# Retention and token/channel mixer on one core: query scaled ahead of the products, sums kept in PSUM, half-array states

## The chip, the core and the metric

The kernel runs on one core of a Trainium2 chip. The core has a matrix engine (PE, which loads a stationary operand and streams a moving one past it, results to PSUM), three engines for elementwise work (DVE, ACT, POOL), a queue engine (SP), an on-chip memory of 128 partitions (SBUF) and eight PSUM banks of 128 partitions x 2 KB. Engines run side by side, each its own instructions in order, and wait for each other by semaphores. The metric is the device time of one execution in microseconds; less is better.

## The reference

Four batches, eight heads of 64, sequence 768. A retention layer with a decaying state per head is followed by a mixer over tokens and then over channels (relu in both, each with a residual):

```
gamma = 1 - 2 ** (-5 - h)                       # per head h
for t in range(768):
    state = gamma * state + outer(k[t], v[t])
    y[t]  = q[t] @ state / sqrt(64)
x  = y, heads side by side                      # (4, 768, 512)
u  = x + (relu(x.T @ w_tok1) @ w_tok2).T        # 768 -> 256 -> 768 over tokens
out = u + relu(u @ w_ch1) @ w_ch2               # 512 -> 1536 -> 512 over channels
```

## The kernel before

The recurrence is done in six chunks of 128 tokens. With gk and gy (powers of gamma inside a chunk, the second with the scale 1/8) a chunk's output is the masked product of its own queries and keys times v, plus its queries times the state that the chunks before it left.

`front(b, p)` does one pair of heads of one batch (16 calls), up to the transposed mixer input:

- The loads bring q, k, v as 16 bit numbers from POOL's queue (L446, L451, L453); `k16` is k times gk, in two halves by head (L500, L502).
- `turn` transposes k and q, in mode "t" or "w" on PE (L526, L528) with a copy from PSUM (L542), or "x" as a DMA on SP (L515). `TURNS` says which for each pair.
- State: five products of a whole chunk's 128 key columns by 128 value columns (L558); only the two 64x64 blocks on the diagonal are wanted. DVE adds them up with decay gp in U, 128 columns wide (L568, L570); L582/L584 copy the two blocks, decayed, into `r16`, whose other blocks are zero.
- Own chunk: six products of 64 partitions for each head (L603), the two heads on the two halves of the array, into four banks; a mask is applied on the way to `am` (L630, or L616 and L621).
- Outputs, in two half sequences: L644 (q times the state, 128 rows) and L647 (mask product times v, 64 columns) sum in a bank; L660/L664 scale by gy into X, L677 casts X to x16.
- Token mixer: L688, relu L697, L713 into new banks; L720 adds to X in place, L728 casts to u16, which is transposed into uT (L747 with copy L753, or L737 on SP).

`back(b)` does the channel mixer: `widen` makes 12 x 2 products of four parts each (L782) with relu on ACT (L798) into h; `narrow7` does the second product for two blocks of 128 tokens by seven half products instead of eight (L857, L872, L889, L905); the last two blocks take the plain `narrow` (L819, L828).

PSUM banks are shared: `first` (pairs of batch 0) any of the eight, `front` banks 0 to 5, `back` 4 to 7.

Order: each piece of work is an `Op` with the engines that could do it, an estimated cost for each, what it depends on and which slots it takes. `arrange` places them in time by these estimates, always the ready one first that ranks first in `PRECEDENCE`, a written-out order of all Ops in base 36. That fixes each engine's order of instructions and, where two engines could do an Op, which does. `ORDER` is the order of the loads. Where the plan leaves PE idle early on, products of zeros (L993) fill 70% of the gap.

Of the kernel before, what the change touches and what calls it, by code (L numbers as in the profile page):

```python
# [91 lines left out]
def arrange(ops, BUFS, BANKS, rank):  # L92
# [158 lines left out]
PRECEDENCE = (  # L251
    "ib89l7she55gqkr3jefy9cua01r20nup4i8rom1du264e9b91rgim2f38v3fmyb265uh27q2sr4c1mmssur5en66gdrgp6iktn9k02jynv4p"
    "et729nbcaj4dc7ow2g0aijo655tcffgjvkr1eo56r89o3q1lj719344n1g4mo1pj883ba6f1wkmwp8pi8gl0uebxlb4hdng83wcydeh3mth0"
    "hdk1j5bt6bgo3js983o081tp8txgcdekl5hqwcma3m7m280ibbkntgank3fqvxbn5br47iaev7dccmdvwbb4985xgmsqcrx53ys5bjm6bu7l"
    "blcugt8no5vb7nrrvmdoe0js8jfirjokcf09v5l6kzwydhins72m9y0ym7rkw9dxj1s1e6ewskq8hpl2brwwwzq16z590vbseampjxcw6q2p"
    "d0e3wrnw9uwjhgprhj62s2iy43sy3em8lv9ilf2cn5hm6sj2ty5f1n7akg8q82gxmni2n72lvjdgad2r060us40hpmis5yceu868hbx9ddx8"
    "fzh66uc0h9osbqwf000f0ewm33tzru8lhxfeudhlm49hmzcibfhffoarrz7shzed3zdsxapb0d04o3ihf8baai99hsmht9k8f43kcpav7bni"
    "ojw39lbvipsoppf98knrclb663b5m37kjlakidccq073gz4v17hohu2wvyiwlrfd1j0rejmi7x97memqlckilw2h8x716ljjoc1ag0w716xd"
    "i76fjd2qthhy1yat7w5ve7onei7znz6dqfm1gs7uvri610lxscopsl8haxtbi95alyivjhh5d81cpl18abugke5dev3uc4hcp2t4pvx6emts"
    "cj3o70401f846pa2erperdoqfm8putju5cbmc6xid7rf80xhd47r3c6i2nxlj4pyasezefwsmfhn0k13ol96vl57i444i3c8rwnyitpko7te"  # L260
    "0zeqjp36aqx4a47ci02aqb6aqqfsbzkm4sfx5448oesm5hcslib08u79ehkyxkft6tw222eg7gwo5mpdcx2vssqapwbko237gko99e5rvglm"
    "3xha0cszd3mj8e1vw6a7xmpxfcwlq56odz9zecg6i1b1lqstamhr126v0ox2mbgfgr7o9gl34anummoi2yqi6hkj50b7c2wiiiva35ctmovz"
    "xe11uj1b3npsjcqybhqgex6986bd7dmdlnd2e1t3d5n8p1nat523hemlpokk31383houic9fka9mve91q33d90rc7jczxjg4klmcdyiopztd"
    "j6qlalnsflrmdmuw2jc3fabg4b77ey1w9x9vpu4wgaqvta92h8lhk94tigsnngr0loilckpntvogn6imkfirbejrj0ixll471kwda0by253s"
    "v4f68zm0j9dbiffbcow5vt6r455jh13iqcvo9w0qja4zf7cajw8aiuodqxrq26034jtqrnu5uq4fkokt8yeusgmxnmlu15w0a8ndtwwta9lp"
    "gwbprsdi08remu3aov1ohhohus619qg73gvhf0vd5prp0l8m5qmvk4pfq6n3g5gv140pm9xbesqnmg2eu4ltse6cg12kqtf2r67tpg0sc9p9"
    "5idunpj34oq941qdncvst8mknxd6c132uztml4jg5278ge8c0gwua1daepljpq6w4rqojih2cn1ix38fqz4ghivuuy5zqraop04649df24qs"
    "nb7407izrxdr7eggrlee2ulan9le76w1a5n1r9quphqewxg98i95sv8o580jdt6xrosbkvjnjzjke8raac5s2i200bjodp1pt7xfu1sdt69t"
    "k6si75ls676k7pc56ne4elq7p4j8qp4epte2oo7q9jk7uk8bl1n4f5u7sa9dub1x2bn0mrfgtfk55krtnlbod1h7g2njwvv1s3gltltx2zo4"
    "cqcv2db3fnchvntu6yjfuv60jt8wgp9bjvdjqjausfu0az1zun2ot0oa3vnqfria9aucq4w8qmtka31ucbk0u63rgqkxhkfk2ft2obfwoyvq"  # L270
    "050wsxumay5t42urr7gcx0o8gnuld9dwawebs6tjrvkr0t5lwhkcrhuuv22tu393wp3lksv9jq87trfhvw4x4u0xvck2wauiotv0gu6jb8vf"
    "9pry53v8t1kw4qlkgbvp4kbw0mpato7vfpl8ofufoxagv6bikughs894aftiu9wgfuuxviqh9r396euoh4lzsjahrb8dri6mfjxcs0ie4y5e"
    "kbttkdlg1en2nti55op51t3pcg6gldht7ykqwedqjm215uwqnkm5khkp7h2xhvg39sozfvor4lpcx1nhjbl91sne3twnx7vv295n2siqdlnf"
    "8s1hsw511qv3dkp385apaaqwnonnp7spgy305w7fi8hww4"
# [4 lines left out]
def kernel(  # L279
# [31 lines left out]
    BUFS = dict(kf=1, k=4, q=4, v=4, k16=3, kT=4, qT=4, U=2, r16=3, am=8, X=3, x16=4, h1=5, u16=3,  # L311
# [14 lines left out]
    HARD = {(0, 0, "k")}  # L326
    ops = []
# [31 lines left out]
    gy = const_p.tile([P, H], FP, name="gy")  # L359
    gp = const_p.tile([P, NP], FP, name="gp")  # L360
    ident16 = const_p.tile([P, P], F16, name="ident16")
    mask = const_p.tile([P, 1, P], FP, name="mask")
    gyw = const_p.tile([P, H, D], FP, name="gyw")
    zero = const_p.tile([P, 384], F16, name="zero")
    NR = BUFS["r16"]
    r16 = [const_p.tile([P, NC - 1, P], F16, name=f"r16_{i}") for i in range(NR)]
# [26 lines left out]
    def emit():  # L393
        for p in range(NP):
            nc.vector.memset(gp[:D, p:p + 1], g128[2 * p])
            nc.vector.memset(gp[D:, p:p + 1], g128[2 * p + 1])
    gp_op = prep("DVE", 600, emit, prio=(-20, 0, -1, 1))
# [3 lines left out]

    def emit():
        for t in r16:
            nc.vector.memset(t, 0.0)
    r16_op = prep("DVE", 1000, emit, prio=(-20, 0, -1, 2))
# [31 lines left out]
    def load(b, p, what):  # L437
# [3 lines left out]
        chunks = what == "q" and not wide  # L441
        s = Slot("kf" if hard else what)

        def emit():
            if wide:
                nc.gpsimd.dma_start(out=tile_of(s, [P, 2, NC, D], F16).rearrange("p h c d -> p h (c d)"),  # L446
                                    in_=src.rearrange("h (p c) d -> p h (c d)", c=NC))
            elif chunks:
                t = tile_of(s, [P, NC, 2, D], F16)
                for j in range(2):  # L450
                    nc.gpsimd.dma_start(out=t[:, :, j], in_=src[j].rearrange("(c p) d -> p c d", p=P))  # L451
            else:
                (nc.sync if hard else nc.gpsimd).dma_start(out=tile_of(s, [P, 2, NC, D], FP if hard else F16),  # L453
                                                           in_=src.rearrange("h (c p) d -> p (h c) d", p=P))
# [4 lines left out]
        else:  # L459
            o = request((-20, 0, b, p), 1660 if chunks else 710 if wide else 1030, emit, dma, [s])  # L460
        loads[b, p, what] = (s, o)

    def front(b, p):
# [10 lines left out]
        def parts(emit, costs, deps, slot, src, steps):  # L474
            got = []
            for st in steps:
                def put(e, st=st):
                    emit(e, st)
                got.append(op(either(put, **costs), deps, [] if got else [slot],
                              ([slot] if got else []) + [src], behind=got[-1] if got else None))  # L480
            return got

        def half(hf):
            return slice(hf * HC, (hf + 1) * HC)

        X, UT = Xs[b], UTs[b]
        pc = slice(p * P, (p + 1) * P)
        (KF, kd), (Q, qd), (V, vl) = (loads[b, p, x] for x in "kqv")
        K = Slot("k16")
# [5 lines left out]
        def emit(e, js):  # L495
            t = opened(K, [P, NC, 2, D], F16)
            for j in js:
                h = 2 * p + j
                if e == "ACT":
                    nc.scalar.activation(t[:, :, j], KF.tile[:, j], AF.Copy, scale=gk[:, h:h + 1])  # L500
                else:
                    (nc.vector if e == "DVE" else nc.gpsimd).tensor_scalar(t[:, :, j], KF.tile[:, j], gk[:, h:h + 1],  # L502
                                                                           None, ALU.mult)
        kl = parts(emit, dict(ACT=(506, 610), DVE=(335 if (b, p, "k") in HARD else 265, 420), POOL=(450, 510)),
                   [kd, g_op], K, KF, ([0], [1]))

        def flat(t):
            return t.rearrange("p c h d -> p (c h d)")

        def turn(src, dst, dep):  # L510
            mode = TURN[b, p, "q" if dst is QT else "k"]
            if mode == "x":
                def emit():
                    t = tile_of(dst, [P, S], F16)
                    nc.sync.dma_start_transpose(out=t.rearrange("d (c t) -> d c t", t=P),  # L515
                                                in_=flat(src.tile))
                o = Op(ops, (PLACE[b, p], 0, b, p, 0), [("SP", 1200, 1200, emit)], dep, [dst], [src], dma=(48, 24))
                return [o, o]
            T = Slot(FA)

            def emit():
                tp = tile_of(T, [P, 1024], F16)
                for c in range(NC):
                    if mode == "w":
                        for j in range(2):
                            nc.tensor.transpose(tp[j * D:(j + 1) * D, c * P:(c + 1) * P], src.tile[:, j, c], ident16)  # L526
# [3 lines left out]
            t = op(one("PE", (465, 530) if mode == "w" else (340, 500), emit), dep + [ident_op], [T], [src])  # L530

            def emit(e, hs):
                d, o = opened(dst, [P, S], F16), T.tile[:, :S]
                if mode == "w":
                    d = d.rearrange("d (f p c) -> d f p c", f=2, c=NC)[:, hs]
                    o = o.rearrange("d (c f p) -> d f p c", f=2, c=NC)[:, hs]
                else:
                    d = d.rearrange("d (f t) -> d f t", f=2)[:, hs]
                    o = o.rearrange("d (f t) -> d f t", f=2)[:, hs]
                if mode == "w" and hs == slice(0, 2):  # L540
                    d, o = d.rearrange("d f p c -> d (f p) c"), o.rearrange("d f p c -> d (f p) c")
                (nc.scalar.copy if e == "ACT" else nc.vector.tensor_copy)(d, o)  # L542
            slow = 1.04 if mode == "w" else 0.54
            if last:
                return parts(emit, dict(ACT=act(SH), DVE=dve(SH, slow)), [t], dst, T,
                             (slice(0, 1), slice(1, 2)))
            return 2 * parts(emit, dict(ACT=act(S), DVE=dve(S, slow)), [t], dst, T, (slice(0, 2),))
        kt = turn(K, KT, kl)
# [85 lines left out]
        for hf in range(2):  # L634
# [35 lines left out]
            if opens:  # L670
                first_of[b, "X"] = ev
# [354 lines left out]
```

## Time and profile before

| | |
|---|---|
| time, median of 3 runs | 196.08 us (195.53 to 196.33) |
| span of the profiled execution | 193.6 us |
| PE, DVE, ACT, POOL busy | 183.6, 146.9, 112.9, 112.4 us |
| products on PE | 2019, of them 35 of zeros |
| granted clock of PE | 1.000 |
| first c1 product (L782) | 31.8 us from the start |
| twentieth | 36.6 us |

The page gives the span, from first to last instruction; the time of an execution also has what lies around it. A PE instruction's length in the records holds its drain, some 0.2 us, which the next one overlaps: the step from start to start says what a product costs.

The costliest groups (line, engine, operation, what from what, shapes, count; busy us and mean ns of one; idle time before, and what ended it) for the lines that the change touches:

```
L660 ACT ACTIVATE X<-bank,gy 128x192 f32<-128x192 f32 x60 | 21.1, 423 | 3.7 <-PE bank L647 2.6
L570 DVE SCALAR_TENSOR_TENSOR U<-U,gp,bank 128x128 f32<-128x128 f32 x64 | 21.9, 342 | 1.7
L720 DVE TENSOR_TENSOR X<-X,bank 128x384 f32<-128x384 f32 x32 | 16.8, 547 | 5.4 <-PE bank L713 5.3
L728 POOL CAST u<-X 128x384 f16<-128x384 f32 x27 | 14.6, 554 | 10.3 <-DVE X L720 10.1
L677 POOL CAST x<-X 128x384 f16<-128x384 f32 x25 | 13.8, 565 | 9.5 <-ACT X L660 9.4
L502 POOL TENSOR_SCALAR k<-k,gk 128x384 f16<-128x384 f16 x10 | 13.8, 1382 | 1.1 <-DMA k<-in_k_dram 0.7
L644 PE MATMUL bank<-r,qT 128*128 128x128 f16 x80 | 12.0, 220 | 0.5 <-ACT r L582 0.2
L647 PE MATMUL bank<-v,am 128*128 128x64 f16 x192 | 13.7, 193 | 0.0
L558 PE MATMUL bank<-v,k 128*128 128x128 f16 x80 | 7.1, 219 | 0.8 <-POOL k L502 0.8
L603 PE MATMUL bank<-qT,kT 64*128 64x128 f16 x192 | 8.6, 218 | 0.4 <-ACT qT L542 0.3 <-DVE kT L542 0.2
```

### The profile page before, as it was taken

The page shows a single profiled execution, that of the slowest core. Times are in us where ns is not written, and L with a number is a line of the kernel's source. Part 1 is how long each engine was busy: PE and PEld are TensorE (multiplying, and loading weights), DVE is VectorE, ACT ScalarE, POOL GpSimd, SP SyncE. Part 2 cuts the span into 40 slices and gives each one's busy share as a digit, 9 for nine tenths or more (in the row PEclk, how much of TensorE's full clock was granted, in tenths as well). Part 3 has the DMA queues.
Part 4 walks back from the last instruction along what each step waited for, and adds up shares of the span by engine and source line. Part 5 has one row for each costly group of instructions (what it writes and reads, how often), then busy time and mean ns, then how long its engine had stood idle before and what let it go on. Part 6 is the DMA issues. An engine that isn't in the chain of part 4 may idle for free.

```text
span 193.6 us, 5153 instructions
## 1 busy us (share of the span) xinstructions
PE 183.6 (95%) x2019; PEld 138.1 (71%) x2019; DVE 146.9 (76%) x387; ACT 112.9 (58%) x261; POOL 112.4 (58%) x157
## 2 busy tenths in 40 slices
PE   7888898989999999999998999999999999999993
PEld 3456687657678977876766898766688877568682
DVE  6699998549989999964498999945195997108792
ACT  3388684997898424688896263448874032672200
POOL 7978978898999794768499949623253000000000
PEclk9999999999999999999999999999999999999999
DMA  6999999999999999999999999952002150200214
GB/s 108 161 163 188 190 206 176 181 193 194 169 146 141 144 138 181 204 149 214 150 125 108 140 127 233 187 164 40 0 5 51 31 220 0 110 3 0 108 59 163
DMA packets 94361, 25.51 MB, mean 132 GB/s; under 512 B 84480, under 2 KB 91392, under 8 KB 94336
## 3 DMA queue, kind: packets, MB, share of 16 engines
q0 software_dynamic: 67584, 13.18, 88.1%
q1 hardware_dynamic: 23152, 5.71, 23.2%
q10 hardware_dynamic: 3600, 6.29, 10.0%
q8 instruction: 16, 0.26, 0.6%
q14 instruction: 9, 0.07, 0.1%
HBM read 26.74 MB, written 6.29 MB: 171 GB/s over the span
## 4 chain that ended last, share of the span: by engine, by line
PE 65%; POOL 13%; DVE 11%; DMA 8%; issue 2%; POOLq 0%; DVEq 0%
PE bank L782 26%; PE bank L872 23%; DMA k<-in_k_dram 6%; POOL k L502 4%; DVE am L630 3%; PE bank L713 3%; PE bank L688 3%; PE bank L819 3%; DMA q<-in_q_dram 3%; DVE U L570 3%; POOL v L453 2%; PE bank L603 2%; PE bank L647 2%; PE bank L644 2%; POOL u L728 1%
## 5 line engine op out<-in xcount | busy, mean ns | idle before, releaser
L782 PE MATMUL bank<-uT,wc 128*128 128x384 f16 x384 | 71.4, 326 | 0.5 <-ACT uT L753 0.5
L798 ACT ACTIVATE h<-bank 128x384 f16<-128x384 f32 x96 | 44.7, 495 | 32.6 <-PE bank L782 25.4
L782 PEld LDWEIGHTS <-wc 128*128 128x128 f16 x384 | 35.5, 98 | 20.2 <-DMA wc<-in_moe_w_ch_dram 0.7
L630 DVE TENSOR_TENSOR am<-bank,mask 128x384 f16<-128x384 f32 x48 | 24.9, 549 | 6.3 <-PE bank L603 6.2
L889 DVE TENSOR_TENSOR X<-X,us 128x256 f32<-128x256 f32 x44 | 18.7, 438 | 12.7 <-ACT us L905 12.6
L872 PEld LDWEIGHTS <-hs 128*128 128x128 f16 x264 | 25.1, 98 | 3.6
L872 PE MATMUL bank<-wsum,hs 128*128 128x256 f16 x198 | 26.4, 273 | 0.0
L660 ACT ACTIVATE X<-bank,gy 128x192 f32<-128x192 f32 x60 | 21.1, 423 | 3.7 <-PE bank L647 2.6
L570 DVE SCALAR_TENSOR_TENSOR U<-U,gp,bank 128x128 f32<-128x128 f32 x64 | 21.9, 342 | 1.7
L889 DVE TENSOR_TENSOR X<-X,bank 128x256 f32<-128x256 f32 x55 | 21.2, 411 | 0.9 <-PE bank L872 0.2
L872 PEld LDWEIGHTS <-h 128*128 128x128 f16 x198 | 19.1, 98 | 3.1 <-issue 0.2
L720 DVE TENSOR_TENSOR X<-X,bank 128x384 f32<-128x384 f32 x32 | 16.8, 547 | 5.4 <-PE bank L713 5.3
L728 POOL CAST u<-X 128x384 f16<-128x384 f32 x27 | 14.6, 554 | 10.3 <-DVE X L720 10.1
L677 POOL CAST x<-X 128x384 f16<-128x384 f32 x25 | 13.8, 565 | 9.5 <-ACT X L660 9.4
L453 POOL DMA_DIRECT2D v<-in_v_dram x16 | 16.8, 1049 | 2.9 <-PE bank L647 1.5
L872 PE MATMUL bank<-wc,h 128*128 128x256 f16 x132 | 17.3, 272 | 0.0
L453 POOL DMA_DIRECT2D k<-in_k_dram x15 | 15.6, 1041 | 0.0
L713 PE MATMUL bank<-h,wt 128*128 128x128 f16 x192 | 14.7, 219 | 0.8 <-ACT h L697 0.5
L502 POOL TENSOR_SCALAR k<-k,gk 128x384 f16<-128x384 f16 x10 | 13.8, 1382 | 1.1 <-DMA k<-in_k_dram 0.7
L647 PE MATMUL bank<-v,am 128*128 128x64 f16 x192 | 13.7, 193 | 0.0
L713 PEld LDWEIGHTS <-wt 128*128 128x128 f16 x192 | 12.0, 98 | 2.3 <-issue 0.6
L647 PEld LDWEIGHTS <-am 128*128 128x128 f16 x192 | 12.1, 98 | 2.1 <-issue 0.5
(69 smaller groups left out, 285.1 us busy)
## 6 DMA issues: line engine op xcount, KB each, us to landing
out_dram<-X ACTq DMA_DIRECT2D x23, 256.0 KB, 2.4
v<-in_v_dram POOLq DMA_DIRECT2D x16, 192.0 KB, 8.4
k<-in_k_dram POOLq DMA_DIRECT2D x15, 192.0 KB, 8.6
wc<-in_moe_w_ch_dram POOLq DMA_DIRECT2D x5, 512.0 KB, 9.3
q<-in_q_dram POOLq DMA_DIRECT2D x8, 192.0 KB, 7.8
q<-in_q_dram POOLq DMA_DIRECT2D x16, 96.0 KB, 9.8
wt<-in_moe_w_tok_dram POOLq DMA_DIRECT2D x2, 384.0 KB, 9.8
wc<-in_moe_w_ch_dram POOLq DMA_DIRECT2D x2, 256.0 KB, 9.6
```

The source lines that it names most:

```text
L453: (nc.sync if hard else nc.gpsimd).dma_start(out=tile_of(s, [P, 2, NC, D], FP if hard else F16), in_=src.rearrange("h (c p) d -> p (h c) d ...
L502: (nc.vector if e == "DVE" else nc.gpsimd).tensor_scalar(t[:, :, j], KF.tile[:, j], gk[:, h:h + 1], None, ALU.mult)
L570: nc.vector.scalar_tensor_tensor(out=u[:, c], in0=u[:, c - 1], scalar=gp[:, p:p + 1], in1=st, op0=ALU.mult, op1=ALU.add)
L630: nc.vector.tensor_tensor(am, src, m, ALU.mult)
L647: nc.tensor.matmul(o[:, j * D:(j + 1) * D], AM[2 * hf + j].tile[:, i], V.tile[:, j, c], start=(c == 0), stop=(c == 0 or j == 1))
L660: nc.scalar.mul(X.tile[:, half(hf), h * D:(h + 1) * D], yv[:, :, j * D:(j + 1) * D], gy[:, h:h + 1])
L713: nc.tensor.matmul(acc[:, i * P:(i + 1) * P], wt2[:, jt, t], H1.tile[:, jt], start=(jt == 0), stop=(jt == NJ - 1))
L720: nc.vector.tensor_tensor(xo, xo, T2.tile[:, :HC * P].rearrange("p (i d) -> p i d", d=P), ALU.add)
L782: nc.tensor.matmul(acc[:, :SH], w[:, ct, (ft % FW) * P:(ft % FW + 1) * P], UT.tile[:, ct, sh * SH:(sh + 1) * SH], start=(ct == 0), stop=(c ...
L798: nc.scalar.activation(H2.tile[:, ft], A.tile[:, :SH], AF.Relu)
L872: nc.tensor.matmul(acc[:, half], l[:, j], r[:, j], start=(j == 0), stop=(j == K2 - 1))
L889: (nc.vector if e == "DVE" else nc.gpsimd).tensor_tensor(dst(), a_(), b_(), ALU.add)
```

## The change

- The query is scaled ahead of its products: pairs whose q is transposed on PE take the factor gq (powers along the token axis, four exponentials on ACT from a second iota) while they are copied from PSUM (on DVE alone); the others are scaled by gy in two halves into q16, as the keys are, and then transposed on SP. Their load is one DMA instead of two. gyw and its work fall away.
- States are kept as two 64x64 blocks: ten products of 64 key columns by 64 value columns instead of five of 128 by 128, into one bank; U and r are 64 columns wide, and r16's zeroed tiles fall away.
- Outputs: one bank per head for the whole sequence. First the twelve products am x v (y0, y1), then ten of 64 partitions and 64 columns for q times the state (y2).
- The second token product is added into the same two banks (24 products of 64 columns instead of 12 of 128), so the bank holds x first and u after. x16 is copied straight from the bank ahead of it; X, and in batch 0 also u16, after it. L660, L677 and L720 have no counterpart; the residual needs no add.
- Key halves: the estimate for POOL rises from 450 to 1200, and other estimates change. PRECEDENCE and the head of ORDER are new; with them the instruction order of every engine is another one, from the first instruction on.

By count: PE 2375 products (38 of zeros); key halves on POOL 0 instead of 10; 71 copies of 384 columns from these banks on ACT and one on DVE. Half-array blocks on PE (runs of products on 64 rows or 64 columns of the array) rise from 26 to 56, 38 of them behind the twentieth c1 product, where 14 were.

```diff
-        def emit(e, js):
-            t = opened(K, [P, NC, 2, D], F16)
...
+        def decayed(tag, src, dep, g, hard):
+            dst, got = Slot(tag), []
+            for j in range(2):
+                def emit(e, j=j):
+                    t, h = opened(dst, [P, NC, 2, D], F16)[:, :, j], 2 * p + j
+                    if e == "ACT":
+                        nc.scalar.activation(t, src.tile[:, j], AF.Copy, scale=g[:, h:h + 1])
+                    else:
+                        (nc.vector if e == "DVE" else nc.gpsimd).tensor_scalar(t, src.tile[:, j], g[:, h:h + 1], None,
+                                                                               ALU.mult)
+                got.append(op(either(emit, ACT=(506, 610), DVE=(335, 420) if hard else (232, 312), POOL=(1200, 1250)),
...
+            if mode == "w":
+                def emit():
+                    d = tile_of(dst, [P, S], F16).rearrange("d (f p c) -> d f p c", f=2, c=NC)
+                    o = T.tile[:, :S].rearrange("d (c f p) -> d f p c", f=2, c=NC)
+                    w = gq[:, p:p + 1].rearrange("d o (p c) -> d o p c", c=NC).to_broadcast([P, 2, SH // NC, NC])
+                    nc.vector.tensor_tensor(d, o, w, ALU.mult)
+                return op(one("DVE", (870, 950), emit), [t, gq_op], [dst], [T])
...
             for c in range(NC - 1):
-                nc.tensor.matmul(st[c // 4][:, c % 4 * P:(c % 4 + 1) * P],
-                                 K.tile[:, c].rearrange("p h d -> p (h d)"), V.tile[:, :, c], start=True, stop=True)
-        pp = op(one("PE", (285, 440), emit), kl + [vl, two_before], ST, [K, V])
+                for j in range(2):
+                    nc.tensor.matmul(st[rows_of(j), c * D:(c + 1) * D], K.tile[:, c, j], V.tile[:, j, c],
+                                     start=True, stop=True)
+        pp = op(one("PE", (290, 450), emit), kl + [vl, two_before], [ST], [K, V])
...
+        def emit(hf):
+            for j in range(2):
+                y = tile_of(Y[j], [P, 512], FP) if hf == 0 else Y[j].tile
                 for i in range(HC):
                     c = hf * HC + i
+                    nc.tensor.matmul(y[:, c * D:(c + 1) * D], AM[2 * hf + j].tile[:, i], V.tile[:, j, c],
+                                     start=(c == 0), stop=False, skip_group_check=True)
+        y0 = op(one("PE", (175, 335), lambda f=emit: f(0)), am_ops[:2] + [vl], Y, [V] + AM[:2])
+        y1 = op(one("PE", (175, 335), lambda f=emit: f(1)), am_ops[2:] + [vl, y0], [], [V] + AM[2:] + Y)
+
+        def emit():
+            for c in range(1, NC):
+                for j in range(2):
+                    nc.tensor.matmul(Y[j].tile[:, c * D:(c + 1) * D], QT.tile[rows_of(j), c * P:(c + 1) * P],
+                                     RS.tile[rows_of(j), c - 1], start=False, stop=False, skip_group_check=True)
+        y2 = op(one("PE", (200, 360), emit), [rs, kt, qt, y0], [], [QT, RS] + Y)
...
+        for j in range(2):
+            x_ops.append(evacuate(X16, Y[j], lambda j=j: opened(X16, [P, NC, 2, D], F16)[:, :, j],
+                                  [y1, y2] + x_ops, [] if x_ops else [X16], ([X16] if x_ops else []) + [Y[j]]))
...
+                        nc.tensor.matmul(Y[j].tile[:, i * D:(i + 1) * D], wt2[:, jt, t],
+                                         H1.tile[:, jt, j * D:(j + 1) * D], start=False, stop=(jt == NJ - 1),
+                                         skip_group_check=True)
+            t2 = op(one("PE", (350, 510), emit), [hr, wops["t2"], x_ops[j]], [], [H1, Y[j]])
...
-    ORDER = ("q00 k00 v00 k01 q01 v01 k02 v02 k03 q02 v03 q03 t1 t2 a0 k10 q10 a3 a2 a1 k11 v10 k12 v11 "
-             "q11 b0 v12 b1 q12 b2 k13 v13 q13 k20 v20 v21 q20 q21 k21 k22 v22 k23 q22 q23 v23 k30 v30 "
-             "q30 k31 v31 q31 v33 v32 k33 q32 k32 q33").split()
+    ORDER = ("q00 k00 k03 v00 k01 q01 k02 q02 t1 v01 q03 t2 v02 a0 v03 k10 a3 q10 a2 a1 k11 v10 k12 q11 "
+             "v11 b0 v12 b1 q12 b2 k13 v13 q13 k20 v20 v21 q20 q21 k21 k22 v22 k23 q22 q23 v23 k30 v30 q30 "
+             "k31 v31 q31 v33 v32 k33 q32 k32 q33").split()
```

## The prediction

> **What bounds the kernel now.** I read the page first: the engines' shares and the chain of waits.
>
> ```profile
> PE 183.6 (95%) x2019; PEld 138.1 (71%) x2019; DVE 146.9 (76%) x387; ACT 112.9 (58%) x261; POOL 112.4 (58%) x157
> ...
> PE 65%; POOL 13%; DVE 11%; DMA 8%; issue 2%; POOLq 0%; DVEq 0%
> ```
>
> PE fills the span and is two thirds of the chain; the granted clock is full throughout. The rest of the chain is POOL, DVE and DMA, so I followed it in order of time to where PE stood still.
>
> ```profile
> 36.86 2.48 POOL k L502 x2
> 39.38 0.51 PE bank L528 x6
> ...
> 51.64 1.26 POOL k L502
> 52.95 0.51 PE bank L528 x6
> ...
> 71.00 0.53 POOL u L728
> 71.57 0.34 PE bank L747 x3
> ...
> 101.16 1.92 POOL k L502
> 103.13 0.45 PE bank L558 x5
> ```
>
> Columns: start, length, what. Four times PE waits for POOL; in three POOL scales a key half (L502, 1.3 to 1.9 us each), in the fourth a cast stands behind one (68.58) and a load's issue. Starts of the PE records give 0.72, 0.30, 0.45 and 0.97 us of standstill, 2.4 in all; from the twentieth L782 product (36.59 us) on, everything else that PE loses outside half-array blocks is 0.9 us.
>
> Next the timeline of PE alone, for the price of a half-array block.
>
> ```profile
> 41.24 1.46 PE L782 MATMUL bank<-uT,wc 128*128 128x384 f16 x8
> 42.64 0.51 PE L603 MATMUL bank<-qT,kT 64*128 64x128 f16 x12
> 43.08 1.15 PE L782 MATMUL bank<-uT,wc 128*128 128x384 f16 x6
> 44.06 0.44 PE L558 MATMUL bank<-v,k 128*128 128x128 f16 x5
> 44.34 0.49 PE L782 MATMUL bank<-uT,wc 128*128 128x384 f16 x2
> ```
>
> Columns: start, length with the last one's drain, line, shape, count. L782 starts every 0.163, so eight should give way at 42.54; L603 begins at 42.64: 0.10 lost on entering. The twelve go two at a time, a pair each 0.056, and should take 0.336; they take 0.44 to the next start: 0.10 lost on leaving (last start to next full start 0.148). L558, full array, takes 0.28 for five (0.056 each), with nothing lost at either end. Other steps read alike: L713 0.0558, L644 0.057, L647 0.0285.
>
> Last the head, by windows (columns: PE, weight loads, DVE, ACT, POOL busy) and ACT's timeline.
>
> ```profile
> 10.00:20.00 10.00, 8.57 (x140) 6.35 (x140) 9.68 (x28) 8.39 (x18) 7.97 (x11) 1.00 1.92 178
> 20.00:30.00 10.00, 9.04 (x158) 7.59 (x158) 9.97 (x24) 7.35 (x17) 8.62 (x13) 1.00 1.42 198
> ```
> ```profile
> 33.99 0.80 ACT L753 COPY uT<-bank 128x768 f16<-128x768 f16 x1 [1.23 <-PE bank L747]
> ...
> 35.21 1.64 ACT L798 ACTIVATE h<-bank 128x384 f16<-128x384 f32 x4
> ```
>
> DVE never rests from 10 to 30 us; PE's busy time there has filler (L993) in it. The head ends when the fourth pair's uT of batch 0 is copied, at 34.79.
>
> **The change, part by part.** The span is 193.6; the median run, 196.08, lies 2.5 above it, and I keep that.
>
> *Half-array blocks.* Per pair, L558 (5 x 0.056 = 0.28) and the five L644 (0.285) each become a block of ten half products of 64 columns. No row of before has this. A block is entry 0.10, four pair steps, and exit. The step lies between 0.0285 (L647, 64 columns) and 0.056 (a pair of 128 columns); the exit between 0.121 (0.148 less the 0.027 that 64 columns fewer stream) and 0.148. So 0.33 to 0.47 a block, +0.10 to +0.37 a pair. Only the 12 pairs after the head count, since PE rests in the head: +1.1 to +4.5. I take 0.030 for the step: at block starts, single records show a half's next weight load 0.028 after its last in L526 (128x64 weights, the state's shape) and 0.015 in L603. That gives 0.10 a pair, +1.2. In the changed order 38 half-array blocks lie behind the twentieth c1 product, where 14 did, and two joints put two of them side by side: -0.2. The second token product becomes 24 x 0.0285 for 12 x 0.0558: +0.2. Sum +1.2.
>
> The Trainium skill, "TensorEngine Tiling (Array Packing)", Restrictions and Gotchas, says that column tiling switches the fast weight load off, and "TensorE: Matmul & The Clock Gate", LDWEIGHTS, puts a slow load at columns / 1.2 ns, estimated 53 ns for the state's 64. By that the state's step would be 0.053 and not 0.030. The 0.028 between loads speaks against it.
>
> *Waits on POOL.* The ten key halves leave POOL (1.38 us each): seven go to DVE (0.53 each), three to ACT (0.62). The 25 x casts on POOL go away, since ACT copies x16 straight from PSUM. Query loads of the later pairs are one issue for two (16 x 0.85 becomes 8 x 1.04). POOL falls from 112 to about 78 us. Of the 2.4 us of standstill I let 0.2 stay: -2.2. If POOL's place is taken by a busy ACT, between 0 and -2.4 stays.
>
> *DVE and ACT.* DVE loses 32 adds of 0.55 (L720), 11 casts and gyw, its 80 U steps are half as wide, and it gains eight products qT of about 0.95 and ten key or query halves: near 126 us. ACT loses L660 (60 x 0.42) and 18 of L582, gains 71 copies of 384 columns and 13 query halves (0.62): near 122. At 65% of the span I cost it nothing outside the head; PE's work hides it. What stands behind an ACT copy is a relu of L798, and behind that PE's next bank: rival three.
>
> *SP.* The eight query transposes of the later pairs now wait for two scaled halves (2 x 0.62 on ACT), and the key and uT transposes stand behind them on SP. PE's idle time before L603 is put down to the switch itself and to DVE and ACT work, to no transpose's landing, so 1.2 us later costs nothing; without that cover it is up to 1.2 at each of eight pairs.
>
> *The head.* A second iota stands ahead of the first load on POOL: 0.23 for 128 columns, so about 0.5 for 384; it pushes every load back by 0.5. The second token weight moves ahead of two v loads (1.3 each): 22.6 - 2.6 + 0.5 = 20.5 landed. From the first u copy, at 20.5 + 0.35, ACT has 27 instructions to the fourth uT: 21 copies of 384 columns at 0.39 (L798 four in 1.64), four of 768 at 0.70, two relus at 0.32, 11.6 us: done at 32.5. The other path: the last v lands where a0 did, 24.0 + 0.5, and state, U (0.25 + 4 x 0.26), r, outputs, two copies, both token products, two copies, transposes and uT add up to 7.9: 32.4. ACT's order will leave it idle some: I take 33.1, in 0.6. The fourteen c1 products behind it put the twentieth at 33.1 + 13 x 0.163 + 0.1 = 35.3, against 36.59: -1.3. Bounds: -2.6 (no push, no idle) and +0.5 (the push alone). By the steps above 0.5 us of product work is issued behind this point that was ahead of it: +0.5. DVE, which had no rest here, has 7.5 (16 masks at 0.47), 5.2 (U), 4.4 (five qT) and some 3 us of halves and copies to do from 8.0 on, and is through at 28. The four exponentials (4 x 0.4), and lnh's memsets (8 x 0.1) fall where ACT and DVE wait for the first key at 4.6 to 5.6 us: nothing, at most 0.5 if the first qT is late for them.
>
> *Sum:* +1.2 - 2.2 - 1.3 + 0.5 = -1.8. Span 191.8, time **194.3**.
>
> **The rivals.**
> One, on the other side: the half-array blocks cost their upper bound. Place: 24 more blocks after the head. Step 0.056, exit 0.148: +4.5 for +1.2, so 197.6. For it: no row has a step below 0.056 in a half-array block. Against: the load spacing. The gains of 3.0 net of the shifted work are used up from 0.25 us a pair on.
> Two: only the state's step is slow, by its weight load (the rule above, as a mechanism of this kernel): 12 x 4 x 0.025 = 1.2 more, 195.5.
> Three: PE waits for banks. Both outputs of a pair stay in PSUM through the two token products, and are let go by ACT copies; the four products before the mask take four of the six front banks, so the next pair's and T1 meet them. For it: ACT did 23.9 us of work between the first and 24th L798 in 25.2. Against: it has 20.9 there now. At 0.15 us a pair, 12 pairs, +1.8: 196.1.
> Four: ACT keeps up in the head and the loads are not pushed: head -2.6, 193.0; with the last POOL waits gone 192.8.
>
> **How the numbers follow.** Chances: forecast 0.40, rival one 0.20, two 0.12, three 0.13, four 0.15. This kernel's runs differ by 0.4%, so I call anything within 0.5% (195.1 to 197.1) the same. The forecast's own range is 193 to 195.5, 0.33 of its 0.40 below 195.1; with rival four 0.15 and 0.02 of two, faster is 0.50. Slower: rival one 0.20 and 0.07 of three, 0.27. The rest, 0.23, is the same. The range reaches from rival four, with something to spare, to rival one: 191.8 to 198.0. As cases of both signs hold much of the chance, the likeliest one's own range stands above.
>
> **What would show it.** The successors of L558 and L644: a block of ten should take 0.33 from its first start to the next full one plus 0.10 ahead; 0.47 makes rival one right, 0.44 in the state's alone rival two. No PE wait on a key scaled by POOL. The twentieth c1 product at 35.3. PE's idle time put down to ACT copies of x or u says rival three. The prediction is wrong if the time between the twentieth c1 product and the end grows by more than 1 us or if the head does not shrink.

## The result, and the profile after

| | before | after |
|---|---|---|
| time, median of 8 runs each | 196.05 us (195.53 to 196.33) | 197.51 us (196.82 to 199.03) |
| ratio, with 95% interval | | 1.0081 (1.0055 to 1.0108) |
| span of the profiled execution | 193.6 us | 196.0 us |
| twentieth c1 product (L782, now L760) | 36.59 us | 37.46 us |
| last start on PE | 189.99 us | 192.39 us |
| between the two | 153.40 us | 154.93 us |

The change makes the kernel 0.8% slower, 1.5 us; a gain of 1.8 was forecast. The spans are of one execution each, and the changed kernel's took 197.98 us, 0.5 above its median, so they lie further apart than the medians do: of their 2.4 us, 0.87 arise before the twentieth c1 product and 1.53 behind it. Medians, ranges and ratios here and below leave out five executions of 198.9 to 202.2 us (one of state_full, three of both_full, one of r_dve), each over 1.5% above the fastest of its kernel, with a mean granted clock of 0.989 to 0.991.

From the page, the shares of the engines and of the chain of waits:

```profile
PE 185.5 (95%) x2374; PEld 137.9 (70%) x2374; DVE 130.6 (67%) x356; ACT 119.8 (61%) x266; POOL 86.5 (44%) x112
...
PE 73%; DVE 9%; DMA 5%; issue 4%; POOL 3%; ACT 3%; POOLq 0%; DVEq 0%
```

POOL has lost 26 us of work and 10 points of the chain, DVE 16 us of work. PE has gained 1.9 us of work and 8 points, and it is PE that sets the end.

PE's waits (what PE stood for and on whom; total us, times, longest):

```profile
PE bank L634 <- POOL r L575: 1.4, 2, 1.0
...
PE bank L524 <- DVE k L500: 1.0, 2, 0.6
...
PE bank L677 <- ACT h L666: 0.7, 1, 0.7
...
PE bank L760 <- DMA uT<-u: 0.5, 1, 0.5
```

No wait for a key on POOL is left, as forecast; keys are now waited for on DVE, in the head. The longest entry shown is a different piece of POOL: r, the decayed state, at line L575. The chain of waits in the head, in order of time (start, length, what), shows where:

```profile
21.49 1.09 POOL r L575
22.62 0.32 PE bank L634 x10
...
28.43 1.09 POOL r L575
29.56 0.35 PE bank L634 x10
29.91 0.47 ACT x L644
30.38 0.38 ACT X L644
30.76 0.38 ACT x L644
31.14 0.40 ACT u L644
31.54 0.38 ACT X L644
31.92 0.39 ACT u L644
32.35 0.51 PE bank L725 x6
```

Twice r takes 1.09 us with the outputs (L634) waiting behind it. Then six copies go one after the other through ACT, where only the x and u copies feed PE and the two X copies stand between them. The source view of r, for the changed kernel (count, then shortest, median and longest in ns, first and last start, shape):

```profile
L575 POOL TENSOR_SCALAR r<-U,gp x11: 1073/1085/1492, 21.5 to 135.4; 128x320 f16<-128x320 f32 x11
```

And for the kernel before, r and, in another line, the key halves on POOL:

```profile
L584 POOL TENSOR_SCALAR r<-U x10: 450/458/647, 18.6 to 134.2; 64x320 f16<-64x320 f32 x10
```
```profile
L502 POOL TENSOR_SCALAR k<-k,gk x10: 1232/1246/1917, 16.2 to 120.6; 128x384 f16<-128x384 f16 x10
```

Both kernels multiply the state by its decay. The old r took a constant; the new one reads its factor from gp, a number for each partition, as the keys do from gk. The operand list shows it: `r<-U` against `r<-U,gp`. By an estimate from the key row, shortened from 384 to 320 columns, the new r takes 1.04 us. The plan did not know it either: the changed kernel's list of costs raises POOL's estimate for a key half to 1200 ns but has 450 for r, and with that the plan gives POOL eleven of the sixteen r.

ACT's timeline in the head (start, length, line, what; idle before and what ended it):

```profile
20.79 0.48 ACT L644 CAST u<-bank 128x384 f16<-128x384 f32 x1 [3.27 <-PE bank L677]
...
22.96 0.48 ACT L644 CAST x<-bank 128x384 f16<-128x384 f32 x1 [0.55 <-PE bank L634]
...
26.04 0.38 ACT L666 ACTIVATE h<-bank 128x256 f16<-128x256 f32 x1 [1.09 <-PE bank L657]
...
35.48 0.80 ACT L731 COPY uT<-bank 128x768 f16<-128x768 f16 x1
```

The first u copy starts at 20.79 (the working gave 20.85), but the fourth uT is done at 36.28, where 33.1 was taken. ACT is idle for 3.0 us in between, not 0.6. It waits for products of PE, of which some stand behind r: with the short r of r_imm below, the same stretch has 2.0 us idle and ends at 35.04.

PE's timeline around the half-array blocks, for the state (L553) and the outputs (L634); the eighteen L760 end by giving way to L626:

```profile
80.72 0.49 PE L760 MATMUL bank<-uT,wc 128*128 128x384 f16 x2
81.14 0.35 PE L553 MATMUL bank<-v,k 128*64 128x64 f16 x10
81.42 0.82 PE L760 MATMUL bank<-uT,wc 128*128 128x384 f16 x4
82.92 0.51 PE L677 MATMUL bank<-h,wt 128*128 128x64 f16 x12 [0.67 <-ACT h L666]
...
88.06 0.34 PE L626 MATMUL bank<-v,am 128*128 128x64 f16 x6
88.33 0.32 PE L634 MATMUL bank<-r,qT 64*128 64x64 f16 x10
88.59 0.35 PE L626 MATMUL bank<-v,am 128*128 128x64 f16 x6
```

By the medians over such blocks, from the starts of the records: the state's block is entered 0.093 us late, runs in pair steps of 0.0375 and is left 0.128 after its last start; 0.372 us in all, where the five full products took 0.280. The outputs' block: 0.097, 0.0325, 0.122, in all 0.349 for 0.285. That is 0.092 + 0.064 = 0.156 a pair, 1.9 us for 12 pairs.

The 0.67 in the fourth line is one of the new standstills. ACT's timeline before it, with ACT's queue of DMA issues:

```profile
79.72 2.71 ACTq L904 DMA_DIRECT2D out_dram<-X  x2
82.48 0.39 ACT L666 ACTIVATE h<-bank 128x256 f16<-128x256 f32 x1 [2.94 <-DVE U L565]
```

ACT issues two stores of outputs; the relu stands behind them, and PE behind the relu. The first issue takes 0.36 us, the second 2.25, to 82.44, although DVE is through with its last add into X before that at 81.14. What holds the issue is not shown: in the profile of r_imm the same issue takes 0.42 us, and this standstill is not there. Standstills of over 0.2 us behind the twentieth c1 product sum to 2.43 us before and to 1.69 after: 0.84 at 81.92 for this relu, 0.63 at 160.91 for a transpose of u on SP, 0.22 at 109.79. The sum differs from one execution to the next: in the profiles of state_full, out_full, both_full, r_imm, q_raw, all_three and pad_out below, which keep this order, it lies between 0.7 and 2.9 us, and the wait near 160 is in all of them but both_full's.

So, behind the twentieth product: +1.9 for the blocks, -0.74 of standstill, +0.5 of work shifted there as forecast make +1.7; the records give 1.53.

### The profile page after: what moved, and what is told of

It reads as the page before. It is cut to its first block, busy times and chain, and to the rows that moved or that the text cites. A ratio compares the mean times of both kernels' runs of the same rounds, so it can differ in the third digit from the quotient of the medians.

```text
span 196.0 us, 5761 instructions
## 1 busy us (share of the span) xinstructions
PE 185.5 (95%) x2374; PEld 137.9 (70%) x2374; DVE 130.6 (67%) x356; ACT 119.8 (61%) x266; POOL 86.5 (44%) x112
## 4 chain that ended last, share of the span: by engine, by line
PE 73%; DVE 9%; DMA 5%; issue 4%; POOL 3%; ACT 3%; POOLq 0%; DVEq 0%
PE bank L760 31%; PE bank L850 20%; PE bank L677 4%; PE bank L657 4%; DMA k<-in_k_dram 3%; PE bank L589 3%; PE bank L797 2%; PE bank L626 2%; DMA uT<-u 2%; DVE U L565 2%; DVE hs L835 2%; PE bank L634 2%; PE bank L553 2%; DVE am L615 1%; POOL r L575 1%
## 5 line engine op out<-in xcount | busy, mean ns | idle before, releaser
L760 PE MATMUL bank<-uT,wc 128*128 128x384 f16 x384 | 69.7, 326 | 0.5 <-DMA uT<-u 0.5
L776 ACT ACTIVATE h<-bank 128x384 f16<-128x384 f32 x96 | 45.2, 494 | 20.5 <-PE bank L760 13.5
L760 PEld LDWEIGHTS <-wc 128*128 128x128 f16 x384 | 34.9, 98 | 20.7
L701 POOL CAST u<-X 128x384 f16<-128x384 f32 x23 | 12.4, 561 | 34.3 <-issue 17.8
L835 DVE TENSOR_TENSOR hs<-h 128x768 f16<-128x768 f16 x18 | 10.1, 568 | 18.7 <-ACT h L776 18.7
L575 POOL TENSOR_SCALAR r<-U,gp 128x320 f16<-128x320 f32 x11 | 13.0, 1179 | 14.7 <-DVE U L565 13.5
L565 DVE SCALAR_TENSOR_TENSOR U<-U,gp,bank 128x64 f32<-128x64 f32 x64 | 17.8, 278 | 1.6
L563 DVE COPY U<-bank 128x64 f32<-128x64 f32 x16 | 3.5, 221 | 20.9 <-PE bank L553 20.7
L644 ACT COPY X<-bank 128x384 f32<-128x384 f32 x31 | 14.2, 485 | 5.4 <-PE bank L677 5.3
L644 ACT CAST x<-bank 128x384 f16<-128x384 f32 x32 | 14.4, 481 | 4.9 <-PE bank L634 2.5
L677 PE MATMUL bank<-h,wt 128*128 128x64 f16 x384 | 15.2, 193 | 0.7 <-ACT h L666 0.7
L677 PEld LDWEIGHTS <-wt 128*128 128x128 f16 x384 | 13.9, 98 | 2.4 <-issue 0.9
L498 ACT ACTIVATE k<-k,gk 128x384 f16<-128x384 f16 x22 | 12.8, 612 | 0.9 <-DMA k<-in_k_dram 0.8
```

The lines of the kernel that those rows point to most:

```text
L498: nc.scalar.activation(t, src.tile[:, j], AF.Copy, scale=g[:, h:h + 1])
L565: nc.vector.scalar_tensor_tensor(out=u[:, c], in0=u[:, c - 1], scalar=gp[:, p:p + 1], in1=st, op0=ALU.mult, op1=ALU.add)
L575: (nc.vector if e == "DVE" else nc.gpsimd).tensor_scalar(r, u, g, None, ALU.mult)
L644: (nc.scalar.copy if e == "ACT" else nc.vector.tensor_copy)(tile(), cols(src.tile[:, :S // 2]))
L677: nc.tensor.matmul(Y[j].tile[:, i * D:(i + 1) * D], wt2[:, jt, t], H1.tile[:, jt, j * D:(j + 1) * D], start=False, stop=(jt == NJ - 1), sk ...
L760: nc.tensor.matmul(acc[:, :SH], w[:, ct, (ft % FW) * P:(ft % FW + 1) * P], UT.tile[:, ct, sh * SH:(sh + 1) * SH], start=(ct == 0), stop=(c ...
```

## The experiments

The theory going in: the blocks cost some 1.8 us (the "drain theory" of the expectations: time lost on entering and leaving a block) and r's operand about 1.0, and these two turn the gain into the loss. The rivals: the transposes on SP, which now wait for scaled queries; the new order; and that neither part matters, because PE would wait for something else. Ratios are to the kernel before on the same chip, with 95% intervals; before's median was 195.76 to 195.85 us in all of them. They need not be the quotients of the medians given beside them; where the two tell different things, the text says so. In state_full, out_full, both_full, r_imm, q_raw and all_three the values computed are not the reference's; they are there for their time alone.

**State by whole chunks again (state_full).** Order and everything else are those of the changed kernel.

```diff
-                    nc.tensor.matmul(st[rows_of(j), c * D:(c + 1) * D], K.tile[:, c, j], V.tile[:, j, c],
-                                     start=True, stop=True)
+                    nc.tensor.matmul(st[:, c * D:(c + 1) * D], K.tile[:, c].rearrange("p h d -> p (h d)"),
+                                     V.tile[:, j, c], start=True, stop=True)
```

> The changed kernel with the state's ten products run on the whole array (128 key columns of both heads as weights, 64 value columns; the second overwrites the first, so the states are not the reference's); instruction counts, order and everything else as in the changed kernel. Drain theory: a state block behind a full-array product takes 0.093 (entry) + 0.151 + 0.128 = 0.372 us now and 10 x 0.0285 = 0.285 then; 12 blocks after the head: -1.0 us, 196.5. Rival (PE is paced by other engines, so time saved on PE is waited away): within 0.3 us of 197.5.

Measured: 196.78 us (196.26 to 198.07, 6 runs), ratio 1.0064 (1.004 to 1.0088). The interval overlaps that of the changed kernel, so the step of about 0.3 us between the ratios is not resolved. In its profiled execution, the chain of waits shows something else:

```profile
86.99 11.30 DMA qT<-q
98.29 0.14 issue
98.43 0.51 PE bank L589 x12
```

One query transpose lies 11.3 us on the chain, and PE stands for 2.28 us ahead of L589. To compare the kernels, I take the stretch from the twentieth product to the last start and leave out the standstills of over 0.2 us: that is 153.2 us in the changed kernel (and also in r_imm and q_raw, which leave the blocks alone) and 152.6 here. So 0.6 us of PE's time is gained, where the theory had 1.0.

**Outputs on the full array (out_full).**

```diff
-                    nc.tensor.matmul(Y[j].tile[:, c * D:(c + 1) * D], QT.tile[rows_of(j), c * P:(c + 1) * P],
-                                     RS.tile[rows_of(j), c - 1], start=False, stop=False, skip_group_check=True)
+                    nc.tensor.matmul(Y[j].tile[:, c * D:(c + 1) * D], QT.tile[:, c * P:(c + 1) * P],
+                                     RS.tile[:, c - 1], start=False, stop=False, skip_group_check=True)
```

> The changed kernel with the ten products of query and state run on the whole array (all 128 rows of qT and r, so each head also gets the other's part and the outputs are not the reference's); all else as in the changed kernel. Drain theory: a block takes 0.097 + 0.130 + 0.122 = 0.349 us now and 0.285 then; 12 blocks: -0.8 us, 196.7. Rival: within 0.3 us of 197.5.

Measured: 197.09 us (196.33 to 197.57), ratio 1.0057 (1.0041 to 1.0073). The stretch behind the twentieth product, standstills left out, is 152.6 us, 0.6 shorter, where the theory had 0.8; in time the intervals again overlap.

**Both (both_full).** The two edits above together.

> Both edits together (values as told for each). Drain theory: the sum, -1.8 us, 195.7, and 24 switches of the array's shape fewer in the trace behind the twentieth c1 product. Rival: above 197.0.

Measured: 196.68 us (194.97 to 197.27, 9 runs), ratio 1.0031 (1.0009 to 1.0053). Its PE timeline at an output block:

```profile
86.06 0.34 PE L626 MATMUL bank<-v,am 128*128 128x64 f16 x6
86.23 0.46 PE L634 MATMUL bank<-r,qT 128*128 128x64 f16 x10
86.53 0.34 PE L626 MATMUL bank<-v,am 128*128 128x64 f16 x6
```

L626 to L634 is 0.17 us here (0.27 in the changed kernel), L634 to L626 0.30 (0.26): ten products on the whole array cost 0.29, and nothing is lost on entering. Of the 38 half-array blocks behind the twentieth product 14 are left, 24 fewer, and the stretch without standstills is 151.9 us: 1.3 shorter, the two single edits together. In time, taking the blocks away gives 0.5% by the ratios, 1.0 us, and the intervals do not overlap; by the medians, each against its own kernel before, it is 0.5 us. The theory of 1.8 had the kind right and the size too high; the runs of this kernel spread over 2.3 us, so the size is not sharp.

**r on POOL with a constant (r_imm).** The two heads of a pair get one decay.

```diff
-                (nc.vector if e == "DVE" else nc.gpsimd).tensor_scalar(r, u, g, None, ALU.mult)
+                if e == "POOL":
+                    nc.gpsimd.tensor_scalar(r, u, g128[2 * p], 1.0, ALU.mult, ALU.mult)
+                else:
+                    nc.vector.tensor_scalar(r, u, g, None, ALU.mult)
```

> The changed kernel with the copy of the state r on POOL multiplied by a constant instead of by a value per partition (the second head of each pair gets the first one's decay); order and engines unchanged. Theory of the head: the copy falls from 1.08 us to about 0.5, as L584's 0.46 on 64 partitions before; two of the copies stand in the head's chain of waits, so the twentieth c1 product comes 1.0 us earlier, at 36.4, and the time is 196.5. Rival (the head hangs on the order of copies on ACT or on loads): the copy is faster but the twentieth c1 product stays within 0.3 of 37.5.

Measured: 195.88 us (195.53 to 198.08, 11 runs), ratio 1.0028 (1.0002 to 1.0054). The source view of its r:

```profile
L576 POOL TENSOR_SCALAR r<-U x11: 449/457/616, 21.5 to 133.4; 128x320 f16<-128x320 f32 x11
```

Same shape, types and engine: 457 ns with the constant, 1085 with a factor for each partition. The twentieth c1 product comes at 36.22, 1.24 earlier, about the 2 x 0.63 that the two r on the head's chain are shorter. That they agree so well is in part luck, since single executions differ: the four other kernels that keep the slow r on POOL (state_full, out_full, both_full, q_raw) have the product at 36.75 to 37.80, all above 36.22. In time the step is 0.5%, 1.0 us, by the ratios, with intervals that just do not overlap, and 1.3 us by the medians: eight of the eleven runs lie at 195.5 to 196.1 us and three at 197.1 to 198.1. This is the clearest of the single edits.

**Transposes from the unscaled query (q_raw).**

```diff
-        def turn(src, dst, dep, mode):
+        def turn(src, dst, dep, mode, raw=None):
...
-                                                in_=src.tile.rearrange("p c h d -> p (c h d)"))
+                                                in_=(raw or src).tile.rearrange("p c h d -> p (c h d)"))
...
-            qt = turn(Q, QT, ql, "x")
+            qt = turn(Q, QT, ql, "x", QF)
```

> The changed kernel with SP's query transposes reading the loaded query and not the scaled one (the scaling still runs on ACT and DVE, its result is unused; eight pairs' queries lack the factor). Theory: since the scaled halves stand in ACT's queue, the third and fourth query transpose are issued at 88.6 and 93.0 us, where before they were at 75.8 and 79.9, and in runs where a transpose takes 11 us and not 6 PE waits for it (2.3 us in one profile); that is why the changed kernel's runs spread over 2.2 us. Then the issue moves to about 86 and 87, the runs spread less, under 1.2 us, and the median falls by 0.3 to 0.8, to about 197.0. Rival (the spread comes from other transposes or loads): spread and median as in the changed kernel.

Measured: 197.38 us (197.14 to 198.34), ratio 1.0096 (1.0077 to 1.0116). The median is not lower than the changed kernel's: the wait of the query transposes for the scaling costs nothing that can be measured. The spread is 1.2 us instead of 2.2, with six runs against eight.

**r on DVE alone (r_dve).**

```diff
-                (nc.vector if e == "DVE" else nc.gpsimd).tensor_scalar(r, u, g, None, ALU.mult)
+                nc.vector.tensor_scalar(r, u, g, None, ALU.mult)
```

> The changed kernel with the eleven copies r that POOL made made by DVE instead (about 0.57 each), the order otherwise the same; the result is the reference's. Theory of the head: as with the constant on POOL, about -1.0, 196.5. Rival: DVE has no room in the head, the twentieth c1 product stays within 0.4 of 37.5.

Measured: 196.97 us (195.91 to 197.16, 5 runs), ratio 1.0054 (1.0033 to 1.0074). DVE does r with the factor per partition in 0.386 us and the twentieth c1 product comes at 36.63, 0.83 earlier; in time only 0.3% is left, inside the intervals, and where the rest goes is not shown. The profiled execution is the one of 202.17 us, so it says nothing on the other five. Its own chain shows a transpose of u on SP (start, length):

```profile
114.67 14.10 DMA uT<-u
```

L760 stands behind it on PE for 3.68 us, and from 128 to 132 us its granted clock is 0.70. The profiled execution of the changed kernel, with the same order of transposes, has no standstill of 0.2 us there.

**Everything that was found (all_three).** state_full, out_full, r_imm and q_raw in one kernel.

> State and output products on the whole array, the constant in POOL's r, and raw queries into SP's transposes, all at once (values as told for each). Theory: the parts add, -1.1 (both blocks) -1.0 (r) -0.5 (queries): 194.9, below the kernel before. Rival (the parts hide one another, or something else is left): 196 or more.

Measured: 195.56 us (194.68 to 196.47, 12 runs), ratio 0.9981 (0.9961 to 1.0001). Against the changed kernel's 1.0081 this is -1.0%, 2.0 us: the 1.0 of the blocks and the 1.0 of r add up (by the medians 0.5, 1.3 and, together, 1.7). Blocks and r account for the loss of 1.5; what is left of the change with both taken out is a gain of 0.2%, not told apart from none, where the forecast had 3.0 net. The profile, of the longest of the twelve runs, confirms the blocks (151.9 us without standstills, as in both_full) but not the head: the twentieth product comes at 37.09, because in this execution PE waits 1.0 us for the first token weight at 17.1.

**The key halves alone: from POOL to DVE (k_dve).** This and k_split start from the kernel before and try the forecast's biggest term by itself.

```diff
-                    (nc.vector if e == "DVE" else nc.gpsimd).tensor_scalar(t[:, :, j], KF.tile[:, j], gk[:, h:h + 1],
-                                                                           None, ALU.mult)
+                    nc.vector.tensor_scalar(t[:, :, j], KF.tile[:, j], gk[:, h:h + 1], None, ALU.mult)
```

> The kernel before with the ten key halves that POOL made emitted on DVE, all else in its order; the result is the reference's. Theory: PE's standstill of 2.4 us behind POOL's key halves goes: 194.2, with the four waits of the chain gone, since 0.53 on DVE replaces 1.38 on POOL. Rival: DVE, 99% busy from 60 to 75 us, hands the wait on, and the time is within 0.6 of 196.

Measured: 196.39 us (195.79 to 197.5), ratio 1.0036 (1.0016 to 1.0057): slower. Standstill behind the twentieth product is 2.85 us, not less than 2.43. PE's waits:

```profile
PE bank L871 <- DVE X L888: 1.4, 3, 0.7
...
PE bank L871 <- DVE hs L856: 0.4, 1, 0.4
```

The chain of waits around the last one, with DVE's adds into X ahead of it:

```profile
69.75 2.06 DVE X L888 x6
...
75.71 0.60 DVE hs L856
76.36 0.83 PE bank L871 x6
```

L871 is a product of the channel mixer, which had nothing to do with the keys. The halves are short on DVE (0.318 us each at the median instead of 1.246), but they stand in DVE's queue with the work that L871 waits for. The wait was passed on, not removed. The time itself is lost elsewhere: from the twentieth product on the stretch is 153.46 us for 153.40, and the twentieth product comes at 37.17 for 36.59. DVE has no rest in the head, and one key half there

```profile
16.40 0.77 DVE L502 TENSOR_SCALAR k<-k,gk 128x384 f16<-128x384 f16 x1
```

moves DVE's queue back by 0.6: its first add into X (L719 here, L720 in the kernel before) starts at 24.49 for 23.92.

**The key halves split between DVE and ACT (k_split).** On top of k_dve's edit the second half of each goes to ACT:

```diff
-                if e == "ACT":
+                if e == "ACT" or e == "POOL" and j == 1:
```

> The kernel before with POOL's ten key halves emitted on DVE (first half) and ACT (second half), all else in its order. Theory left after the same edit with DVE alone: the standstill behind POOL is one of several chains of the same length, and the wait goes where the work goes; 195.8 to 196.5, PE's standstill behind the twentieth c1 product between 2 and 3 us again. Rival (DVE alone was the wrong place): standstill under 1.2 us and 194.8 or less.

Measured: 194.85 us (194.5 to 195.65), ratio 0.9954 (0.9939 to 0.9969), faster than the kernel before and the changed one. From its page:

```profile
PE 183.2 (95%) x2019; PEld 138.1 (72%) x2019; DVE 146.8 (76%) x392; ACT 114.6 (59%) x266; POOL 98.6 (51%) x147
```

POOL is 13.8 us emptier, DVE no fuller than before (146.9), ACT fuller by 1.7. The standstill is 1.72 us, 0.7 less than before, and the twentieth product to the end is 152.2 for 153.4. So the keys on POOL were worth 0.9 us in time, not 2.2, and only with the work spread over two engines. The time is at the rival's bound, and the theory of no gain falls; the standstill lies between the two.

**The outputs on the whole array with zeroed tiles (pad_out).** r goes in two halves, by constants, into tiles that are zero elsewhere, as before the change; the state stays in half-array blocks. The core of the edit:

```diff
-            r, u, g = tile_of(RS, [P, NC - 1, D], F16), US.tile, gp[:, p:p + 1]
...
+            for j in range(2):
+                r, u, g = RS.tile[rows_of(j), :, j], US.tile[rows_of(j)], g128[2 * p + j]
+                if e == "ACT":
+                    nc.scalar.mul(r, u, g)
+                else:
+                    (nc.vector if e == "DVE" or j else nc.gpsimd).tensor_scalar(r, u, g, 1.0, ALU.mult, ALU.mult)
...
+                    nc.tensor.matmul(Y[j].tile[:, c * D:(c + 1) * D], QT.tile[:, c * P:(c + 1) * P],
+                                     RS.tile[:, c - 1, j], start=False, stop=False, skip_group_check=True)
```

> The changed kernel, correct, with r in tiles that are zero outside the two heads' blocks and made in two halves by a constant (one on POOL and one on DVE where POOL made it, both on ACT or on DVE where these did), so that the outputs' ten products run on the whole array without a switch. Theory: -0.5 (as the output blocks on the whole array measured) and -0.8 in the head (0.46 beside 0.4 for 1.08): 196.2, near the kernel before. Rival: the second instruction per copy costs on DVE and ACT what it saves, within 0.5 of 197.5.

Measured: 197.67 us (197.26 to 197.96), ratio 1.0095 (1.008 to 1.0109): no gain. Each half costs 0.447 us on POOL and 0.482 on DVE, so DVE has 13 instructions for r where it had one, and the standstill rises to 2.62 us. The twentieth product comes at 37.26, 0.2 earlier and not 0.8. What the whole array saves PE is there (152.4 us without standstills, 0.8 less) but is not seen in the time.

**No written-out order (no_order).** PRECEDENCE is empty, so that the planner's own priorities decide.

```diff
-PRECEDENCE = (
...
+PRECEDENCE = ""
```

> The changed kernel with an empty PRECEDENCE, so that the Ops rank by their own priorities. It tells how much the written-out order is worth here: theory, several per cent, 203 to 212 us, most of it as PE standing still; rival, under 2 us, and then the new order cannot be what makes up for the switches.

Measured: 197.46 us (197.17 and 197.76, two runs), ratio 1.0086 (1.0064 to 1.0109), the same as the changed kernel. Here the written-out order is worth nothing that two runs could show; the rival of under 2 us is right, the theory of 203 to 212 far off.

## Why the prediction was wrong

A span shorter by 1.8 us was forecast and one longer by 2.4 came. Of these 4.2 us the head makes 2.2, the waits on POOL 1.5 and the blocks 0.7, together 0.2 too much.

- *Half-array blocks, +1.2: the mechanism was right, the term was sized low.* Entry 0.10 was taken and 0.093 to 0.097 measured; the step 0.030 and 0.0325 to 0.0375; the exit, taken at its lower bound of 0.121, is 0.122 for the outputs and 0.128 for the state. Together 0.156 a pair on PE, 1.9 us in all. The working wrote 0.10 a pair, where its own values give 0.12 (a block of 0.341, two of them for 0.565), so 0.2 of the miss of 0.7 is a slip in the sum. Taking the blocks away gives back 1.3 us of PE's time and, by the ratios, 1.0 us of time.
- *Rivals one and two: wrong.* With its entry a block takes 0.372 and 0.349 us, where the working had 0.33, rival one 0.47 and rival two 0.44 for the state alone (the prediction's last part sets the entry beside the 0.33 once more, though the working has it within). The step is far from 0.056. That the time fell near rival one's 197.6 is chance: the blocks cost 1.9 us and not 4.5, and the head and the waits made up the rest. The state's step is longer than the outputs', but by 0.005 us and not by rival two's 0.025. On that rule the Trainium skill, "TensorEngine Tiling (Array Packing)", Restrictions, says that column tiling disables the fast weight load. The traces do not show whether the 0.005 us come from it.
- *Waits on POOL, -2.2: this step failed.* The four waits that it named are gone, but the sum of standstills fell by 0.74 only: a relu behind the issue of ACT's stores and a DMA of u came in. Part of this is chance of the execution (in r_imm's profile the relu's 0.84 is not there), but no profile with this order has less than 0.7 left. I had let 0.2 stay because PE no longer waited for POOL, without asking what the work does to the engine that takes it over. k_dve shows that answer alone (2.85 us left, and a later head), k_split that spreading it is worth 0.9.
- *The head, -1.3: this step failed, by 2.2 us (37.46 for 35.3).* From the landing of the last v (23.99) to the fourth uT (36.28) it took 12.3 us, where the working had 7.9. (The twentieth product is less late than this uT, since the last fourteen c1 products start at 35.28, ahead of its end.) The one mis-sized term that was tried is r, for which the working gives no price of its own: I had taken L584's 0.46. With the gp operand it is 1.085, on the chain twice; r_imm gives 1.24 of the 2.2 back. POOL's total says the same: 86.5 us busy where the working had 78, with 13.0 us of r for 4.9 before. The other 0.9 I read from the chain and did not try: ACT is idle for 3.0 us where I took 0.6, X copies stand between the x and u copies that PE waits for, and DVE does two key halves (0.86 and 0.23 us on the chain from 26.47 on) ahead of the U that the second r needs. The last is like what k_dve shows in the old kernel: key halves on DVE hold its queue back in the head. The push of 0.5 by the second iota did not come: the last v landed at 23.99 where 24.5 was taken, the second token weight at 19.99 for 20.5.
- *Shift of +0.5, second token product, joints:* agree with the ledger of 1.53 us behind the twentieth product within 0.2; not tested alone.
- *Queries on SP, nothing:* right in the median, by q_raw.
- *Rival three, banks held by copies of x or u:* wrong; no product's wait of 0.2 us or more is put down to a copy of L644, and of the weight loads' only two, of 0.3 us each. *Rival four* is wrong with the head.
- *What would show it* did: the two signs that the prediction named for being wrong, a growth of more than 1 us behind the twentieth product and a head that does not shrink, both came.

Open: how much of the blocks' 1.9 us is hidden, and why (1.3 came back on PE, 1.0 in time, the latter with an uncertainty of about 0.7 from the two intervals); the head's other 0.9; and what the slow store issue and the late transposes in single executions come from.

## What to carry to other kernels

Price an instruction by its operands too: the same multiply on POOL was 0.46 us with a constant and 1.09 with a factor per partition, and the row with the right price was in the old profile under another line. A plan that chooses engines by estimates needs that price as well: here it had 450 ns for r. A short block of ten products on a part of the array cost some 0.2 us for entering and leaving, more than it saved in streaming. And a wait for an engine is won only if the work finds a place that nothing stands behind: moved to DVE alone it was lost, split between DVE and ACT it paid 0.9 us.

## What was not expected of the hardware

- POOL's multiply by a factor for each partition takes 2.4 times that by a constant (1085 and 457 ns, 128x320); DVE does the first in 386.
- Products of 64 columns on halves of the array go two at a time, a pair each 0.0325 us on row halves and 0.0375 on column halves, against 0.0285 for one on the whole array: the pair costs little more than one, but the switches take it back.
- A transpose by DMA took up to 14.1 us from issue to landing in one execution and a median of 4.8 to 8.2 in others of kernels with the same order. The kernels built on the changed one spread over 0.7 to 2.6 us with five runs or more, the kernel before over 0.8 to 1.4.
